# Attention and two MoE layers on one core: keys and queries loaded in 2 KB pieces, keys of two heads laid side by side on the chip, another order in the last step

## The chip, the cores and the metric

One core of one Trainium2 chip. The metric is the device time of one execution in microseconds (us); what stands for a kernel is the median of its runs. The core's engines are PE (matrix products), DVE (vector), ACT (scalar and activation), POOL (general) and SP (here it only issues transfers); 16 DMA engines move data.

## The reference, cut to what matters

Inputs q, k and v have the shape (2, 8, 768, 64): 2 batches, 8 heads, 768 positions, 64 numbers a head. All is float32.

```
k_sum = max of k over blocks of 32 positions        # 24 a head
v_sum = mean of v over blocks of 32 positions
scores_l = q @ k.T / 8, kept where |i - j| < 16
scores_s = q @ k_sum.T / 8 + log(32)
a = softmax over [scores_l, scores_s];  attn = a @ [v, v_sum]
x = attn as (1536, 512)
p = domain_probs / row sum
x = sum over 4 experts of p[:, e] * (relu(x @ w1[e]) @ w2[e])
P = 8 rounds of row and column scaling of exp(x @ w_gate - max)
out = sum over 8 experts of P[:, e] * (relu(x @ w1b[e]) @ w2b[e])
```

w1 has the shape (512, 1024) for each expert, w2 (1024, 512). The output has the shape (1536, 512).

## The kernel before, in words

**Attention.** The 16 heads are taken as 8 pairs (`pairs`). For pair i, `add_loads` (L1024) issues on SP: k of both heads (L1031), q of both heads (L1038), v (L1045), and windows of v (L1057). K lands with a position a partition, so a run of 256 B; q with two positions a partition, 512 B. There are two buffers for each of k, q and v, used in turn. `add_keys` (L1067) turns k over on PE (7 transposes of 128 columns, two halves of which one block is common), so that both heads' 64 numbers lie on 128 partitions and positions along the columns; ACT copies one half into `kw`, DVE the other (L1097 to L1101): 12 tiles of 96 positions, overlapping, each followed by 24 columns for the block maxima. DVE takes the maxima (L1106) and spreads them over the tiles (L1120). `add_queries` (L1130) turns q over and writes the scaled queries into `bd`, every second column for each of the two positions of a partition (L1147). `add_values` (L1160) makes the block means of v on POOL and PE. `add_group` (L1195) does 4 tiles at a time: scores on PE, maximum on DVE, exponentials on ACT, sum on DVE, product with 1/sum on POOL (L1250), transposes on PE, their copy on ACT, product with v on PE, and the copy into the layer's input `xf`. There are 24 such groups. `add_x` (L703) makes from `xf` the seven operands of the first product, each split in two parts (hi on ACT, L463; lo on DVE or POOL, L458 and L453).

**MoE.** A unit is 256 of an expert's 1024 hidden columns; there are 16 units in the first layer and 32 in the second, and for each unit two steps, b = 0 and 1, one for each batch: 96 steps. A step has a first product (`add_first`, L510; matmuls L303), a hop in which the hidden values become seven split operands (`add_hop`, L564), and a second product (`add_second`, L603; matmuls L612) that is added into `acc`. Each product uses seven products of quarter blocks in place of eight, named by digits: `FIRST` and `SECOND` (L1368, L1369) give their order for each b. Digit 2 is A12 B21, 3 is S4 B22, 4 is A22 N4, 7 is S3 T3. Each of the seven is 6 matmuls in the first product and 3 for each half dc in the second. `add_weights` (L465) loads a unit's weights, sums blocks of them by accumulating DMAs from POOL (L498) and splits them. At the border between the layers `add_turn` (L735) makes the next input; after expert 0 of the second layer `add_scale` (L769) applies its weights. `add_out` (L911) adds up, turns over and stores.

**Order.** Nothing runs in the order of the text. Each piece is an `op` (L358) with an engine, a planned time from `SPAN` (L330), what it reads and writes, and a due time. `run_work` (L377) plays all engines forward with these times and always emits the piece that can start first, the smaller due time deciding among equals. That fixes the order on every engine, SP and POOL queues included. Instructions marked `shared` (SBUF to SBUF on DVE and POOL) are planned one at a time. Constants at L1370 to L1386 shift due times: `ALONG` for the attention as a whole, `AHEAD` for its loads, `W0DUE` and `WAIT0` for the first unit's weights, `LEAD2` for the splits, `SOONER` and `LATER` for the steps about the border, `NARROW` for the pair from which three PSUM banks are left to the MoE.

Of the kernel before, what the change touches and what calls it, by code (L numbers as in the profile page):

```python
# [18 lines left out]
def local_global_attention_moe_moe(  # L19
# [14 lines left out]
    P = 128  # L34
# [98 lines left out]
    PB = [xp.tile([P, BLK], F32, name=f"pb{b}") for b in range(2)]  # L133
# [10 lines left out]
    KT = 7  # L144
    KA, KB = KT * KX, (NQ - KT) * KX
# [12 lines left out]
    def view_vs(t):  # L158
        return t.rearrange("x (t j d) -> x t j d", j=2, d=D)

    kns = [
        t.rearrange("x (c j d) -> x c j d", j=2, d=D)
        for t in (quads[:, 0:BLK], put("h0", BLK, "kn"))
    ]
    qns = [
        t.rearrange("x (j c d) -> x j c d", j=2, d=2 * D)
        for t in (quads[:, BLK:2 * BLK], put("h1", BLK, "qn"))
    ]
    vns = [t.rearrange("x (h c d) -> x h c d", h=2, d=D) for t in (PB[1], put("h2", BLK, "vn"))]
# [10 lines left out]
    ks = [accs[1][:, 2 * NB_ + i * NS:2 * NB_ + (i + 1) * NS] for i in range(2)]  # L180
    vbs = [accs[1][0:KX, 2 * NB_ + (i + 1) * P:2 * NB_ + (i + 2) * P] for i in range(2)]
# [17 lines left out]
    HOP_AT = {B11: "h0", N1: "h1", B21: "h2", B22: "h3", N2: "h3", T3: "h5", N4: "h5"}  # L199
# [15 lines left out]
    def x_of(b, c, r, i):  # L215
        if (b, c) != (1, 1):
            return xop[b, c][r][:, i]
        if (i, r) not in x11:
            tag = X_AT[i]
            group = [x for x in range(NOP) if X_AT[x] == tag]  # L220
            if tag == "xc":
                x11.update(operand("x11c", tag, group, (0, 1)))
            else:
                x11.update(operand(f"x11{tag}{r}", f"{tag}{r}", group, (r,)))
# [91 lines left out]
    def relu(S, out, src, th, neg=False):  # L316
# [12 lines left out]
    ADD = 0.85  # L329
# [6 lines left out]
        "v1536": (1.3, 1.34), "vmax": (0.57, 0.65), "vsum": (0.57, 0.66), "vrec": (0.12, 0.18),  # L336
        "vks": (0.6, 0.69), "vksw": (0.600001, 0.69), "vks2": (0.35, 0.42), "vkw": (0.7, 0.81), "vq": (1.0, 1.1),
# [4 lines left out]
        "p256": (0.75, 0.77), "p384": (1.05, 1.08), "psm": (0.98, 1.02), "pks": (0.8, 0.85),  # L342
        "pid": (0.55, 0.6), "p1": (0.2, 0.25), "pmask": (3.0, 3.1), "psel": (0.9, 0.95),
        "add1": (0.95, 1.3, ADD, 1.2), "add2": (0.950001, 1.3, 2 * ADD, 1.2),
        "addx": (0.950003, 1.3, 1.5 * ADD, 1.2), "add3": (0.950002, 1.3, 3 * ADD, 1.2), "ld": (0.45, 1.0, 0.65, 1.3),
        "st": (0.450001, 0.5, 0.5, 1.2), "ldk": (0.550002, 1.1, 1.2, 1.2),
# [256 lines left out]
    def add_second(n):  # L603
# [897 lines left out]
```

## Time and profile before

| | us |
|---|---|
| median of 3 runs | 1543.28 (1543.21 to 1543.91) |
| the profiled execution's own time | 1539.3 |
| its span, first to last instruction | 1537.3 |
| busy: PE, DVE, ACT, POOL | 1507.2, 1373.2, 1137.7, 486.1 |
| granted PE clock, mean | 0.999 of full |

Each row of a window gives its length, for every engine the busy time and in brackets the number of instructions, the granted clock, the busy share of the 16 DMA engines (it can be over 1, since packets overlap) and GB/s. In a row by line `out<-in` names the tiles, then come partitions x elements; behind the bar stand busy us and the mean of one in ns. The chain of waits follows the work that ended last back to what released it.

### The profile page before, as it was taken

Reading aid. Unit: us, or ns where it says so; the run is one execution under the profiler, and the core shown is the slowest. Engines: PE = TensorE matmul, PEld = TensorE weight load, DVE = VectorE, ACT = ScalarE, POOL = GpSimd, SP = SyncE. Lnnn points to the kernel's source line nnn. Section 1 sums busy time; section 2 is a strip of 40 time slices with the busy share of each in tenths; the row PEclk is TensorE's granted clock in tenths of the full one; section 3 lists DMA queues with packets and bytes.
Section 4 is the critical chain, followed back from the end, with each engine's and each line's share of the span. In section 5 each row is a group of like instructions: output and inputs, shape, how many; then the busy total and the mean of one; then the engine's idle time right before and its main releaser. Section 6 shows DMA issues by size and latency. Waiting matters only on the chain.

```text
span 1537.3 us, 26618 instructions
## 1 busy us (share of the span) xinstructions
PE 1507.2 (98%) x9058; PEld 1481.4 (96%) x9058; DVE 1373.2 (89%) x2842; ACT 1137.7 (74%) x2443; POOL 486.1 (32%) x513
## 2 busy tenths in 40 slices
PE   7989999999999999999999999999999999999997
PEld 6889999999999988998999999999999999999996
DVE  7987999899889896999989899899899899899987
ACT  5988777777677788767677677677777777777764
POOL 4643323323322341343232323323332323233220
PEclk9999999999999999999999999999999999999999
DMA  9977666566566683597567566667567566567632
GB/s 216 230 131 141 123 132 129 112 131 130 107 133 134 111 156 70 102 173 150 100 121 149 106 122 140 114 119 142 110 124 144 106 126 139 111 120 136 120 62 89
DMA packets 199032, 196.51 MB, mean 128 GB/s; under 512 B 46432, under 2 KB 157424, under 8 KB 198896
## 3 DMA queue, kind: packets, MB, share of 16 engines
q0 software_dynamic: 82944, 116.42, 47.6%
q1 hardware_dynamic: 115952, 78.39, 18.5%
q8 instruction: 71, 1.16, 0.3%
q14 instruction: 65, 0.53, 0.1%
HBM read 73.97 MB, written 3.22 MB: 50 GB/s over the span
## 4 chain that ended last, share of the span: by engine, by line
PE 89%; DVE 5%; DMA 2%; ACT 2%; POOL 1%; issue 1%; SPq 0%; DVEq 0%; POOLq 0%; ACTq 0%
PE bank L303 44%; PE bank L612 43%; DVE acc L238 1%; DVE hoph L458 1%; DMA pb<-prow 1%; PE bank L800 0%; ACT s L1235 0%; DVE acc L244 0%; POOL s L1250 0%; ACT xhi L463 0%; DMA pb<-in_v_dram 0%; DMA raw<-in_moe_w_dram 0%; DMA raw<-raw 0%; DMA acc<-acc 0%; DVE quads L320 0%
## 5 line engine op out<-in xcount | busy, mean ns | idle before, releaser
L612 PE MATMUL bank<-hoph,w2hi 128*128 128x384 f32 x2688 | 687.8, 336 | 7.4 <-ACT bank L623 5.8
L612 PEld LDWEIGHTS bank<-hoph,w2hi 128*128 128x128 f32 x2688 | 483.5, 188 | 14.2 <-ACT bank L623 9.8
L612 PE MATMUL bank<-hoph,w2lo 128*128 128x384 f32 x1344 | 449.5, 334 | 0.0
L238 DVE TENSOR_TENSOR acc<-bank,acc 128x384 f32<-128x384 f32 x730 | 386.4, 553 | 14.9 <-PE bank L612 13.1
L463 ACT ACTIVATE hoph<-quads 128x384 fp32r<-128x384 f32 x672 | 335.0, 522 | 61.5 <-PE bank L612 36.8
L458 DVE TENSOR_TENSOR hoph<-quads,hoph 128x384 fp32r<-128x384 f32 x583 | 313.1, 555 | 36.7 <-ACT hoph L463 36.6
L303 PE MATMUL bank<-xhi,w1hi 128*128 128x384 f32 x1008 | 338.6, 336 | 1.9 <-DVE quads L320 1.9
L303 PE MATMUL bank<-xlo,w1hi 128*128 128x384 f32 x1008 | 337.3, 335 | 0.0
L303 PE MATMUL bank<-xhi,w1lo 128*128 128x384 f32 x1008 | 337.0, 334 | 0.0
L498 POOL DMA_DIRECT2D raw<-raw x195 | 198.5, 1029 | 363.6 <-DMA raw<-raw 146.6
L623 ACT COPY bank<-bank 128x384 f32<-128x384 f32 x384 | 180.9, 471 | 116.0 <-PE bank L612 110.2
L612 PEld LDWEIGHTS bank<-hoph,w2lo 128*128 128x128 f32 x1344 | 252.3, 188 | 0.2 <-DMA w2lo<-xf 0.2
L303 PEld LDWEIGHTS bank<-xhi,w1hi 128*128 128x128 f32 x1008 | 189.2, 188 | 3.9 <-DVE quads L320 2.6
L303 PEld LDWEIGHTS bank<-xhi,w1lo 128*128 128x128 f32 x1008 | 189.2, 188 | 0.1
L303 PEld LDWEIGHTS bank<-xlo,w1hi 128*128 128x128 f32 x1008 | 189.3, 188 | 0.0
L498 POOL DMA_DIRECT2D xf<-xf x93 | 95.7, 1029 | 176.3 <-DMA xf<-xf 75.1
L623 ACT COPY bank<-acc 128x384 f32<-128x384 f32 x174 | 83.5, 480 | 86.0 <-DVE acc L238 84.9
L623 ACT COPY acc<-bank 128x384 f32<-128x384 f32 x218 | 103.7, 481 | 47.6 <-PE bank L612 43.2
L491 POOL DMA_DIRECT2D w2lo<-raw x66 | 69.7, 1056 | 182.4 <-ACT w2lo L488 178.3
L320 DVE SCALAR_TENSOR_TENSOR quads<-bank,pb 128x384 f32<-128x384 f32 x178 | 99.0, 556 | 21.9 <-PE bank L303 16.2
L582 DVE SCALAR_TENSOR_TENSOR quads<-quads 128x384 f32<-128x384 f32 x192 | 106.3, 554 | 1.5
L241 DVE TENSOR_TENSOR quads<-quads 128x384 f32<-128x384 f32 x185 | 102.6, 555 | 2.0 <-ACT quads L318 0.5
(190 smaller groups left out, 1904.1 us busy)
## 6 DMA issues: line engine op xcount, KB each, us to landing
raw<-raw POOLq DMA_DIRECT2D x130, 256.0 KB, 4.0
raw<-in_moe_w_dram SPq DMA_DIRECT2D x66, 256.0 KB, 2.8
raw<-in_moe_w_dram SPq DMA_DIRECT2D x128, 128.0 KB, 3.1
xf<-xf POOLq DMA_DIRECT2D x62, 256.0 KB, 3.8
w2lo<-raw POOLq DMA_DIRECT2D x33, 384.0 KB, 4.8
w1lo<-raw POOLq DMA_DIRECT2D x32, 384.0 KB, 4.0
pb<-prow SPq DMA_DIRECT2D x24, 384.0 KB, 3.8
w2lo<-raw POOLq DMA_DIRECT2D x33, 256.0 KB, 3.8
```

The source lines that it names most:

```text
L238: (eng or nc.vector).tensor_tensor(out=out, in0=x, in1=y, op=ALU.add)
L241: (eng or nc.vector).tensor_tensor(out=out, in0=x, in1=y, op=ALU.subtract)
L303: nc.tensor.matmul(pm, l[:, s, cs_], x_of(b, c, r, x), start=first and i == 0, stop=i == n - 1, skip_group_check=True,)
L320: nc.vector.scalar_tensor_tensor(out=out, in0=src, scalar=0.0, in1=PB[S[1]][:, th * HB:(th + 1) * HB], op0=ALU.min if neg else ALU.max, op ...
L458: e.tensor_tensor(out=out, in0=src, in1=hi.bitcast(F32), op=ALU.subtract)
L463: aop(lambda: nc.scalar.mul(to(0), src, -1.0 if neg else 1.0), reads, writes, due, "ah")
L491: lambda: nc.gpsimd.dma_start(out=l, in_=src, accum_op=ALU.add),
L498: lambda o=o, x=x: nc.gpsimd.dma_start(out=o, in_=x, accum_op=ALU.add),
L582: nc.vector.scalar_tensor_tensor(out=q[o], in0=q[x], scalar=-1.0, in1=q[y], op0=ALU.mult, op1=ALU.subtract)
L612: nc.tensor.matmul(cut[bank], l[:, s, cols], hop_of(t, r), start=start and i == 0, stop=i == 2, skip_group_check=True,)
L623: aop(lambda: nc.scalar.copy(out=out, in_=src), [kin], [kout], due)
```

## The change

K is loaded as q and k lie in memory, 8 positions (2 KB) a partition on 96 partitions, into one staging buffer `kst`; two copies, on DVE for the first pair and on POOL for the others, lay the two heads side by side in `kn`; PE makes 8 transposes of 96 columns, in two halves of 4; ACT copies one half to `kw` and DVE the other. Since a transposed column block holds every 8th position, the copies write every 8th element. The maxima are taken in two halves, and one instruction merges and spreads them. Q is loaded likewise, turned over in 2 x 4 transposes of 96 columns and scattered with the same step. `kst`, `kn` and `qn` have one buffer each. `kn` lies in the place of the two weighting rows `pb`, v's first buffer moves to `quads`, and the operand N1 of the hop moves from `h1` to `h0`.

Further: b = 1 gets other orders in `FIRST` and `SECOND`, the second product of the last step the order `FINAL`; one subtraction of `add_turn` for each half (b = 1, operand 6) goes to POOL; planned times and due times change, which changes the order everywhere. `BYPOOL` is empty, so its two branches never run. The diff, cut:

```diff
+    pbs = xp.tile([P, 2 * BLK], F32, name="pb")
+    PB = [pbs[:, b * BLK:(b + 1) * BLK] for b in range(2)]
...
+    RW = 8
+    RP, NR = S // RW, 2 * RW * D
...
+    kst = put("h0", NR, "kst")[0:RP].rearrange("x (j r d) -> x j r d", j=2, d=D)
+    kn = pbs[0:RP, 0:NR].rearrange("x (r j d) -> x r j d", j=2, d=D)
+    qn = quads[0:RP, 0:NR].rearrange("x (j r d) -> x j r d", j=2, d=D)
...
-    ADD = 0.85
+    ADD = 1.0
...
-        "st": (0.450001, 0.5, 0.5, 1.2), "ldk": (0.550002, 1.1, 1.2, 1.2),
+        "ld": (0.45, 1.0, 0.65, 1.3), "ldr": (0.55, 1.1, 1.75, 1.3),
+        "st": (0.450001, 0.5, 0.5, 1.2), "ldk": (0.550002, 1.1, 0.57, 1.2),
...
-    HOP_WAIT = 0.09
+    HOP_WAIT = 0.08
...
-            for j, m in enumerate(SECOND[b]):
+            for j, m in enumerate(SECOND[b] if n < NST - 1 else FINAL):
...
-                lo_op("DVE", to, src, [key, k + (0,)], [k], d, neg)
+                eng = "POOL" if (b, i) in TURNPOOL and not neg else "DVE"
+                lo_op(eng, to, src, [key, k + (0,)], [k], d, neg)
...
-                    out=kn[:, :, j, :], in_=k[b, 2 * hp + j].rearrange("(c p) d -> p c d", p=P)
+                    out=kst[:, j], in_=k[b, 2 * hp + j].rearrange("(p r) d -> p r d", r=RW)
...
-                    in_=q[b, 2 * hp + j].rearrange("(c p r) d -> p c (r d)", p=P, r=2),
+                    out=qn[:, j], in_=q[b, 2 * hp + j].rearrange("(p r) d -> p r d", r=RW)
...
+            op(
+                "POOL" if i and KPOOL[j] else "DVE", "pkj" if i and KPOOL[j] else "vkj",
+                [("kst", j)],
+                [("kn", j)], d - 0.01,
+                lambda j=j: (nc.gpsimd if i and KPOOL[j] else nc.vector).tensor_copy(
+                    out=kn[:, :, j], in_=kst[:, j]
+                ),
+                True,
+            )
...
+                for r in range(n):
+                    nc.tensor.transpose(
+                        full[tk["bank"]][:, r * RP:(r + 1) * RP],
+                        kn[:, r0 + r].rearrange("x j d -> x (j d)"), ident[0:RP, 0:RP],
+                    )
...
+                copy = nc.vector.tensor_copy if half else nc.scalar.copy
+                to = t[:, :, 0:KW].rearrange("x t (m r) -> x t r m", r=RW)
+                w = KW // RW
+                for src, st, tiles in (
+                    ((QT - WIN) // RW, QT // RW, slice(1, NQ - 1)),
+                    (0, (S - KW) // RW, slice(0, NQ, NQ - 1)),
+                ):
+                    o = to[:, tiles, r0:r0 + n, :]
...
+            a, b_ = (x[:, None, :].to_broadcast([P, NQ, NS]) for x in ks[p])
+            nc.vector.tensor_tensor(out=t[:, :, KW:KX], in0=a, in1=b_, op=ALU.max)
...
-                        t[j * D:(j + 1) * D, :, j, r:QT:2],
+                        t[j * D:(j + 1) * D, :, j].rearrange(
+                            "x t (q c r) -> x r c t q", r=2, c=RW // 2
+                        )[:, r],
...
-    FIRST = {0: "1562734", 1: "1567342"}
-    SECOND = {0: "1256437", 1: "1524637"}
-    HOP, GOFF, DCOFF, LEAD, LEAD2 = 1.11, 0.15, 6.7, 1.0, 0.94
+    FIRST = {0: "1562734", 1: "1567234"}
+    SECOND = {0: "1256437", 1: "1526437"}
+    FINAL = "1562743"
+    HOP, GOFF, DCOFF, LEAD, LEAD2 = 1.11, 0.15, 6.7, 1.0, 0.53
...
-    AHEAD = 3.8
-    ALONG = 7.5
-    NARROW = 7
-    WAIT0 = 1
-    KSPOOL = False
-    XDUE = [-2.5, -1.7, -0.9, 0.3]
-    W0DUE = -4.8
-    FIRST0 = -1.3
+    BYPOOL = ()
+    ALONG = 5.2
+    NARROW = 6
+    WAIT0 = 3
+    KPOOL = (True, True)
+    AHEAD, VAT, SAT = 6.3, 0.3, 0.86
+    XDUE = [-2.6, -1.7, -0.9, -0.5]
+    W0DUE = -2.1
+    FIRST0 = 0.2
...
+    TURNPOOL = ((1, 6),)
```

`LATER`, `SOONER` and `XPOOL` get other values too, and more of the planned times.

## Rows read from the trace of the kernel before

**Rows 1.** Busy time of each engine, page, part 1: us, share of span.

```profile
PE 1507.2 (98%) x9058; PEld 1481.4 (96%) x9058; DVE 1373.2 (89%) x2842; ACT 1137.7 (74%) x2443; POOL 486.1 (32%) x513
```

**Rows 2.** Windows of the second MoE layer: length, busy us (instructions), clock, DMA.

```profile
700.00:720.00 20.00, 18.92 (x105) 17.60 (x104) 19.92 (x43) 14.27 (x30) 7.23 (x8) 1.00 0.84 162
740.00:760.00 20.00, 20.00 (x117) 20.00 (x116) 18.68 (x38) 16.84 (x37) 4.69 (x5) 1.00 0.57 122
```

**Rows 3.** Windows of the attention, same columns.

```profile
0.00:30.00 30.00, 21.55 (x177) 18.29 (x178) 20.44 (x49) 15.36 (x41) 12.40 (x30) 1.00 1.08 212
30.00:60.00 30.00, 29.38 (x325) 26.08 (x324) 27.50 (x70) 28.11 (x83) 18.40 (x19) 1.00 1.12 240
60.00:90.00 30.00, 24.51 (x301) 20.88 (x299) 27.85 (x61) 25.30 (x74) 19.81 (x21) 1.00 0.94 176
90.00:110.00 20.00, 19.41 (x145) 18.00 (x146) 18.25 (x34) 18.45 (x41) 6.62 (x7) 1.00 0.69 131
```

**Rows 4.** Chain of waits, 0 to 110 us: start us, us, what.

```profile
26.38 5.21 DMA raw<-in_moe_w_dram
31.61 3.95 DMA acc<-in_v_dram
...
85.22 5.08 DMA raw<-raw
```

**Rows 5.** Timeline of PE, same stretch: start, us, line, [idle before].

```profile
4.77 1.73 PE L1077 MATMUL bank<-ident,quads 128*128 128x128 f32 x7 [4.77 <-POOL sel L985]
...
89.92 0.44 PE L303 MATMUL bank<-xhi,w1hi 128*128 128x384 f32 x1
```

**Rows 6.** DMA issues, 0 to 100 us: count, KB each, median us to landing.

```profile
quads<-in_k_dram SPq DMA_DIRECT2D x8, 192.0 KB, 5.0
```

**Rows 7.** DMA packets of 8-10, 2-4, 28-30, 31-33, 1522.5-1526 us; last line: queue.

```profile
DMA packets 1400, 0.35 MB, mean 176 GB/s; under 512 B 1400, under 2 KB 1400, under 8 KB 1400
DMA packets 1762, 0.50 MB, mean 248 GB/s; under 512 B 1552, under 2 KB 1762, under 8 KB 1762
DMA packets 763, 0.57 MB, mean 287 GB/s; under 512 B 44, under 2 KB 763, under 8 KB 763
DMA packets 684, 0.61 MB, mean 305 GB/s; under 512 B 60, under 2 KB 497, under 8 KB 684
DMA packets 491, 0.92 MB, mean 264 GB/s; under 512 B 47, under 2 KB 47, under 8 KB 490
q1 hardware_dynamic: 490, 0.91, 69.2%
```

**Rows 8.** DVE by line, 0 to 92 us: shapes, count | busy, mean ns.

```profile
L1147 DVE TENSOR_SCALAR bd<-bank 64x384 f32<-64x384 f32 x8 | 4.4, 546 | 0.1
L1097 DVE COPY kw<-bank 128x384 f32<-128x384 f32 x4 | 2.2, 550 | 0.4 <-PE bank L1077 0.4
L458 DVE TENSOR_TENSOR xlo<-acc,xhi 128x384 fp32r<-128x384 f32 x6 | 4.5, 747 | 1.3 <-ACT xhi L463 1.3
L453 DVE SCALAR_TENSOR_TENSOR xlo<-acc,xhi 128x384 fp32r<-128x384 f32 x1 | 0.5, 544 | 0.0
```

**Rows 9.** POOL by line, 0 to 92 us.

```profile
L1250 POOL TENSOR_TENSOR s<-s,sm 128x480 f32<-128x480 f32 x24 | 25.0, 1056 | 28.9 <-DVE sm L1245 13.8 <-ACT acc L1285 5.3 <-ACT s L1265 3.2
L238 POOL TENSOR_TENSOR pb<-pb 128x384 f32<-128x384 f32 x4 | 4.5, 1135 | 2.7 <-DMA pb<-in_v_dram 2.7
```

**Rows 10.** ACT by line, 0 to 92 us.

```profile
L1147 ACT ACTIVATE bd<-bank 64x384 f32<-64x384 f32 x8 | 4.1, 515 | 1.3 <-PE bank L1139 1.1
L1097 ACT COPY kw<-bank 128x576 f32<-128x576 f32 x4 | 2.6, 661 | 5.2 <-PE bank L1077 3.8 <-DVE acc L1106 1.4
```

**Rows 11.** Chain of waits, 1490 to 1538 us.

```profile
1511.10 0.56 DVE quads L320
...
1516.37 0.99 ACT hoph L463 x2
...
1528.65 0.53 DVE acc L629
```

More of the change, by code (lines that the diff above doesn't have):

```diff
@@ L481, in group @@
             aop(lambda: nc.scalar.copy(out=h, in_=src), rd, [key + ("hi",)], due, span)
+            if (kind, u) in BYPOOL:
+                op(
+                    "POOL", f"p{n * FU}", rd + [key + ("hi",)], [key + ("lo",)], due + 0.05,
+                    lambda: vsub(l, src, h.bitcast(F32), nc.gpsimd), True,
+                )
+                return
             if by_dve:
@@ L495, in add_weights @@
         for o, x, wr, rd in sums_of(kind, u):
+            if (kind, u) in BYPOOL:
+                op(
+                    "POOL", f"p{len(wr) * FU}", [R[j] for j in (*rd, *wr)], [R[j] for j in wr],
+                    start + 0.5, lambda o=o, x=x: vadd(o, o, x, nc.gpsimd), True,
+                )
+                continue
             op(
@@ L906, in add_row @@
         op(
-            "SP", "ld", [f"prow{layer + 1}"], keys, due,
+            "SP", "ldr", [f"prow{layer + 1}"], keys, due,
             lambda: load_row(out, layer, e, b),
@@ L1103, in maxima, with copies @@
-            def maxima(half=half, c0=c0, nh=nh, tk=tk):
+            op("PE", "kt4", [("kn", 0), ("kn", 1), "ident"], key, e, turn, take=tk)
+            def copies(half=half, r0=r0, tk=tk):
+                pt = full[tk["bank"]]
+                copy = nc.vector.tensor_copy if half else nc.scalar.copy
[6 more added lines that the diff above has]
+                    o = to[:, tiles, r0:r0 + n, :]
+                    copy(
+                        out=o,
+                        in_=bass.AP(
+                            pt.tensor, pt[:, src:src + 1].offset,
+                            [list(pt.ap[0]), [st, o.shape[1]], [RP, n], [1, w]],
+                        ),
+                    )
@@ L1115, in add_keys @@
                 vop(copies, key, [("kw", p, 1)], e, "vkw", False, use=tk)
[L1116 removed]
+            vop(maxima, key, [("ks", p, half)], e, "vks", False, use=tk)
         def spread():
[L1119 to L1128 removed]
+            a, b_ = (x[:, None, :].to_broadcast([P, NQ, NS]) for x in ks[p])
+            nc.vector.tensor_tensor(out=t[:, :, KW:KX], in0=a, in1=b_, op=ALU.max)
+        vop(spread, [("ks", p, 0), ("ks", p, 1)], [("kw", p, 2)], d + 0.03, "vksw", True)
     def add_queries(i, d):
@@ L1350, in set_places @@
         for key in QUAD:
-            over[key] = [(x, 0, j) for x in ("kn", "qn") for j in range(2)]
-        over["pb", 1] = [("vn", 0)]
+            over[key] = [("qn", 0), ("qn", 1), ("vn", 0)]
         for i in range(NOP):
@@ L1418, in local_global_attention_moe_moe @@
                     add_x(b, c, XDUE[i // 2])
+        for b in range(2):
+            over["pb", b] = [("kn", 0), ("kn", 1)]
         op(
-            "SP", "ld", ["prow1", ("mark", 4)], [("pb", 0)], A0 + 14 * AD,
+            "SP", "ldr", ["prow1", ("mark", 4)], [("pb", 0)], A0 + 14 * AD,
             lambda: load_row(PB[0], 0, 0, 0),
```

131 lines of the change are left out of this document (50 added, 81 removed), and 2 rows, old and new, of the table SPAN.

## Prediction

> **What bounds the kernel now.** I read the page's busy shares first, then the windows by stage, then the chain of waits, then the DMA view, and last the groups by line of the engines that the change touches.
>
> The busy shares put PE at 98% of the span [rows 1], but that is an average over stages. The windows show them apart. A full stretch of the MoE has PE at 20.00 of 20 us with 117 matmuls [rows 2]; nothing that spares DMA, DVE or ACT can shorten it. Time can be won only where PE runs short: in the attention at the front, around the border between the layers and at the weighting step of the second layer, and in the tail.
>
> In the attention PE, DVE and the DMA engines share the blame. From 0 to 110 us DVE is busy 94.04 us, so it sits idle for 15.96 us; 9.56 us of that lies in the first 30 us, 4.65 us in the next 60 [rows 3]. DMA stands at 94 to 112% of the 16 engines over the first 90 us [rows 3] (above 100% because packets overlap on an engine). So the loads gate the first third, and DVE (27.5 and 27.9 us of 30) the other two. The chain of waits says the same: three of its longest pieces in this stage are transfers, one of them the weights of the first unit, loaded between the third and the fourth pair of heads, with a window load of v behind it, and one the sum of that unit's weights, which ends just after the first MoE product has started at 89.92 us [rows 4, 5].
>
> **Part 1: K and Q in 2 KB pieces.** Each of the 16 K and 16 Q issues moves 192 KB, K rows of 256 B and Q rows of 512 B (one of four such rows is shown [rows 6]): 6.29 MB in 18432 packets; afterwards 3072 packets of 2 KB. The rate before: a stretch with nothing but 256 B packets moves 176 GB/s, one with mostly K from 256 B rows 248 GB/s, one with 512 B and larger pieces 287 GB/s [rows 7]. K's 3.15 MB thus take 12.7 to 17.9 us; Q's 3.15 MB lie between 248 and 287 GB/s, 11.0 to 12.7 us. Together 23.7 to 30.6 us. The rate after: nearest are a stretch with 2 KB weight rows among others, 305 GB/s, and the stores of 2 KB rows, 0.92 MB in 3.5 us with a third of the stretch idle, so at 69.2% busy some 380 GB/s [rows 7]. That gives 16.6 to 20.6 us. The saving in transfer time is 3.1 to 14.0 us; I take 9, near the middle, because the windows that run beside the K loads are the 256 B kind and slow them. The saving is on the path as long as the transfers gate, which is the first third and parts of the rest.
>
> **Part 2: the copy that lays two heads side by side.** Two copies of 512 elements for each pair. For the first pair they run on DVE: with 0.55 us for 384 elements [rows 8], 0.73 us each, 1.5 us in all, on the path of the first transposes; K landing sooner and PE's start, which now waits on POOL's mask work until 4.77 us [rows 5], cover about 1 us. For the other seven pairs POOL does them: 14 copies. The nearest rows are POOL's two-operand instructions of 384 and 480 elements, 1.14 and 1.06 us [rows 9]; I take 1.1 us, 15 us in all. POOL is busy 50.6 of the first 90 us [rows 3], so they fit, up to 66. What they cost is contention: where POOL works beside it, DVE's subtraction takes 747 ns, its like 544 ns [rows 8]. Six rows at 0.2 us over their like are 1.2 us; 15 us on top of POOL's 50.6 raise that by a third, and other DVE lines have their share, so 0.4 to 2 us; I take 1. Behind a copy that waits for its K stand on POOL the products of the softmax (24 of 1.06 us [rows 9]), for which PE's transposes wait. Only one K stage and one Q buffer remain, so the next load can't start until the copy, or Q's transposes, are through; a K transfer lands 5.0 us after issue [rows 6] and a pair takes some 10 us, so I take 0, with up to 2 us as the bound.
>
> **Part 3: the scatter on the chip.** PE turns 8 + 8 blocks of 96 columns where it turned 7 + 6 of 128: 1536 columns for 1664, nothing. The maxima read 768 columns as before (2 x 384 for 512 + 256). DVE's share of the keys grows from 480 to 576 columns, 96/384 of 0.55 us, 0.14 us for each pair, and the spread becomes one instruction instead of two; I take 0. The copies of keys and the scaled queries now write every 8th element, 32 B apart, where keys were contiguous and queries 8 B apart. The trace prices the 8 B step: 384 elements take 546 ns with it and 550 ns without on DVE, and on ACT 515 ns with it [rows 8, 10]. A step of 32 B is not in it. Its cost lies between 0 and a doubling of those rows; I take 0, since the only stepped rows at hand cost nothing. The doubling is the third rival.
>
> **Part 4: order.** The first unit's weights wait for the fourth pair's K (WAIT0 3) and are due later, which takes the piece at 26.38 us out of the attention's way [rows 4]. What is late next is their sums: already now their last transfer ends only as the first products run [rows 4, 5]. Part of the 5 us won at 26 us may be given back there; I leave both inside the sum below. The dues of row loads, of POOL's accumulating DMAs and of the splits also move everywhere, which in the full stretches can gain nothing and lose up to 2 us.
>
> **Part 5: border and weighting.** DVE is busy 19.92 of 20 us while PE makes 105 matmuls instead of 117 [rows 2]. Two subtractions of 0.55 us go from DVE to POOL at the border: at most 1.1 us; I take 0.5, between 4 gained and 4 lost for the new order.
>
> **Part 6: the tail.** In the last step PE runs dry at 1511.1, when the gate of the product A12 B21 starts; all hop operands hang on it, and from there DVE and ACT work until 1517.4 [rows 11]. With the new order two products of 1.04 us follow this gate instead of none, so the chain starts 2.1 us sooner. FINAL ends with c12, which needs one instruction before the transposes, instead of c22, which has one of 0.53 us [rows 11] and two more of such length behind it: up to 1 us. I take 2.5 of these 3.1; bounds 4.5 gained (the ACT copy that waits on a store goes too) and 1 lost.
>
> **The sum.** In the attention the gain is what DVE's idle 15.96 us can give back. Some of it must stay: the loads still start from nothing, and the softmax's chain is serial. I take half, 8.0 us, after the 1 us of part 2; transfers save about as much (9). So 8.0 + 0.5 + 2.5 = 11.0 us. The profiled execution has a time of 1539.3 us (its span is 1537.3), 4.0 us under the median of 1543.28; I take that offset as unchanged, so 1543.3 - 11.0 = 1532.3 us.
>
> **Rivals.**
> 1. *All idle goes.* With quick loads the first MoE products, which need only the first half of the pairs, fill PE while DVE finishes: 16.0 + 0.5 + 2.5 = 19.0 us, 1524.3 us. For it speaks that PE, too, has idle in the attention; against it, DVE's 27.9 of 30 us [rows 3].
> 2. *The loads were hidden.* From 30 us on DVE is the limit anyway [rows 3], or the weight sums hold the first product [rows 4]; only parts 5 and 6 remain: 3.0 us, 1540.3 us. Against it speaks the idle 9.56 us of the first 30.
> 3. *Slower: the 32 B step.* If a write with this step takes twice as long, DVE pays for 576 + 768 elements per pair, 3.5 x 0.55 = 1.93 us, 15.4 us over eight pairs, and ACT 0.66 + 2 x 0.515 = 1.69 us, 13.5 us [rows 8, 10]. Then the sum is -11.0 + 15.4 = +4.4 us, 1547.7 us; it turns at 11.0 us, a factor of 1.7. Against it speaks that the 8 B step is free; for it, that nothing wider was run here. The Trainium skill (SBUF — State Buffer, section on Door 1, the DMA port swizzle) bears on this: "So how far you can stride for free depends on dtype: 4 fp32, 8 bf16, 16 int8." By that rule a step of 8 elements pays and one of 2 doesn't; the free 8 B rows agree with it, but no row decides about 32 B; were its price the doubling, the time would be this rival's.
>
> **How the numbers follow.** Forecast 0.60, its own range 1527 to 1537; rival 1 0.15, rival 2 0.13, rival 3 0.12. About 0.2%, 3.1 us, is what a measurement of this kernel can tell from no change. Forecast and rival 1 are faster (0.75), rival 2 lies at the edge and counts as same (0.13), rival 3 is slower (0.12). The range 1524 to 1544 holds all but rival 3 and what lies below rival 1.
>
> **What would show it.** Right: the DMA view counts about 1536 packets each for K and Q; the DMA share in the first 80 us falls below 100%; DVE's idle in 0 to 110 us falls to about 8 us; the first product of L303 starts near 82 us instead of 89.92 [rows 5]; the last one before the final transposes comes some 2 us closer to the end. Wrong: the key copies and scaled queries take over 0.9 us for 384 elements (rival 3); the product starts after 87 us though the loads are through early (rival 2); the POOL copies stand waiting for K with softmax products behind them; PE falls under 117 matmuls per 20 us between 120 and 540 us.

## The result: slower, and the profile after

The changed kernel takes 1552.85 us (median of 5 runs, 1551.88 to 1560.63), the kernel before, run beside it on the same chip, 1543.71 us (5 runs, 1543.21 to 1544.54). The ratio is 1.0074, 95% interval 1.0055 to 1.0093: slower by 9.1 us by the medians and 11.4 by the ratio, where 11 us of gain were forecast. The profiled execution of after took 1551.88 us with a span of 1550.0 us.

The busy shares (page, part 1) hardly differ from [rows 1]:

```profile
PE 1512.8 (98%) x9082; PEld 1484.9 (96%) x9082; DVE 1372.6 (89%) x2835; ACT 1138.7 (73%) x2443; POOL 497.8 (32%) x528
```

As before, the answer lies in the stages. The windows of after, same columns as [rows 2, 3]:

```profile
0.00:30.00 30.00, 21.11 (x178) 18.50 (x178) 23.38 (x45) 16.86 (x38) 15.83 (x35) 1.00 1.00 208
30.00:60.00 30.00, 27.74 (x326) 24.15 (x324) 27.79 (x57) 27.33 (x74) 17.41 (x21) 1.00 1.03 230
60.00:90.00 30.00, 25.98 (x264) 22.65 (x262) 25.50 (x54) 26.14 (x63) 21.24 (x23) 0.89 0.84 174
90.00:110.00 20.00, 17.78 (x166) 14.98 (x162) 18.37 (x37) 17.38 (x47) 10.93 (x11) 1.00 0.51 102
...
740.00:760.00 20.00, 20.00 (x118) 20.00 (x117) 18.34 (x37) 14.07 (x30) 4.23 (x6) 1.00 0.50 93
840.00:860.00 20.00, 17.67 (x93) 17.34 (x92) 14.17 (x30) 12.31 (x26) 7.10 (x7) 0.91 0.66 125
```

Two things are to be seen. In the first 30 us DVE is 3 us busier than in [rows 3] and yet runs fewer instructions (45 for 49): its instructions got longer. And a stretch in the middle of the second layer, 840 to 860 us, has 93 matmuls where a full one has 117 [rows 2], at a granted clock of 0.91.

DVE, ACT and POOL by line, 0 to 95 us (columns as in [rows 8 to 10]); these answer to the key copies and scaled queries there:

```profile
L1115 DVE COPY kwxa<-bank 128x480 f32<-128x480 f32 x4 | 4.1, 1026 | 0.0
L1115 DVE COPY kwxa<-bank 128x96 f32<-128x96 f32 x4 | 1.4, 343 | 0.0
L1115 ACT COPY kwxa<-bank 128x480 f32<-128x480 f32 x4 | 4.2, 1061 | 1.3 <-DVE acc L1126 1.2
L1168 DVE TENSOR_SCALAR bd<-bank 64x384 f32<-64x384 f32 x8 | 6.8, 854 | 0.1
L1168 ACT ACTIVATE bd<-bank 64x384 f32<-64x384 f32 x8 | 6.9, 863 | 0.2
L1085 POOL COPY pb<-kst 96x512 f32<-96x512 f32 x14 | 8.6, 626 | 2.9 <-DMA kst<-in_k_dram 2.8
L1085 DVE COPY pb<-kst 96x512 f32<-96x512 f32 x2 | 0.8, 417 | 0.0
```

A scaled query of 384 elements takes 854 ns on DVE and 863 on ACT; with the 8 B step of before it took 546 and 515 [rows 8, 10]. That is 1.57 and 1.68 times. The copies that lay two heads side by side are cheap: 626 ns on POOL, 417 on DVE.

PE's timeline, 60 to 100 us: the first MoE product (L299, before L303) starts at 92.32 us, 2.4 us later than in [rows 5]:

```profile
68.46 2.06 PE L1236 MATMUL bank<-kwxa,acc 128*128 128x120 f32 x8 [1.56 <-DVE kwxa L1143]
...
92.32 0.33 PE L299 MATMUL bank<-xhi,w1hi 128*128 128x384 f32 x1
```

The DMA issues of 0 to 100 us, first after, then the rows of before that stand beside the one in [rows 6]:

```profile
kst<-in_k_dram SPq DMA_DIRECT2D x16, 192.0 KB, 5.1
quads<-in_q_dram SPq DMA_DIRECT2D x16, 192.0 KB, 4.1
```

```profile
quads<-in_q_dram SPq DMA_DIRECT2D x8, 192.0 KB, 4.4
...
kn<-in_k_dram SPq DMA_DIRECT2D x8, 192.0 KB, 6.5
qn<-in_q_dram SPq DMA_DIRECT2D x8, 192.0 KB, 4.6
```

The pieces are as planned: the page counts 183672 packets for 199032, and the difference of 15360 is exactly 18432 less 3072. The loads of the same 192 KB land little sooner: K 5.1 us after its issue (median), where it took 5.0 into one buffer and 6.5 into the other, Q 4.1 us, where it took 4.4 and 4.6.

**Where the time went.** I counted the matmuls of the two products (L299 and L621) up to a given moment in both traces; one takes 0.174 us. After lags before by 6.9 us at 120 us, 7.8 at 540, 7.5 at 720, 11.8 at 860, 15.3 at 1500, and the spans differ by 12.7. Between these two profiles the attention lost 7 us, the first layer and the border nothing more, the second layer's full stretches 7.8, and the tail gave 2.4 back: from the last first product to the end it is 23.88 us, before 26.23. One caution: the profiled execution of before was 4.0 us faster than its median, that of after 1.0, so some 3 us of this lag are those of the two executions. Two kernels that are as fast as before by their medians (2 and 3 below) show where they lie: counted alike, the profile of b_order lags 1.9 us at 120 us, that of b_kq1536 2.8, and their first products start at 91.97 and 92.85 us. So 4 to 5 of the attention's 7 us belong to the change, and a first product at 92.32 us is no sign of a loss by itself.

The waits of 720 to 1480 us (engine, buffer and line, what it waited for: us in total, times, longest us) show what stops the second layer; before had no wait of PE there, and none of ACT's splits for a sum:

```profile
ACT w1hi L478 <- DMA raw<-raw: 7.5, 5, 3.1
...
PE bank L621 <- ACT bank L632: 4.8, 5, 2.3
ACT w1hi L478 <- DMA xf<-xf: 1.6, 1, 1.6
```

and the timeline at 840 us shows one of them:

```profile
840.33 1.20 POOL L507 DMA_DIRECT2D raw<-raw  x1 [3.96 <-DMA raw<-raw]
...
844.22 0.62 ACT L478 CAST w1hi<-raw 128x512 fp32r<-128x512 f32 x1 [3.10 <-DMA raw<-raw]
844.87 0.69 DVE L237 TENSOR_TENSOR w1lo<-raw,w1hi 128x512 fp32r<-128x512 f32 x1 [2.54 <-ACT w1hi L478]
845.49 0.47 ACT L632 COPY bank<-bank 128x384 f32<-128x384 f32 x1
...
846.01 0.96 PE L621 MATMUL bank<-hoph,w2hi 128*128 128x384 f32 x2 [2.33 <-ACT bank L632]
```

POOL stood 3.96 us for one sum before it issued the next; the split of the weights on ACT waited 3.10 us for that one; and behind the split, in ACT's order, stood the bank copy for which PE's second product waits, 2.33 us. The split itself is not urgent, but it blocks the queue. PE's waits make 5.1 of the 7.8 us. Right behind this wait the granted clock is 0.76 and 0.81 in the 8 us from 844 us, which by estimate (the missing share of each 4 us) is up to 1.7 us more.

### The profile page after: what moved, and what is told of

Read it like the earlier page. It is cut to its first block, busy times and chain, and to the rows that moved or that the text cites. A ratio compares the mean times of both kernels' runs of the same rounds, so it can differ in the third digit from the quotient of the medians.

```text
span 1550.0 us, 26653 instructions
## 1 busy us (share of the span) xinstructions
PE 1512.8 (98%) x9082; PEld 1484.9 (96%) x9082; DVE 1372.6 (89%) x2835; ACT 1138.7 (73%) x2443; POOL 497.8 (32%) x528
## 2 busy tenths in 40 slices
DMA packets 183672, 196.51 MB, mean 127 GB/s; under 512 B 34144, under 2 KB 138992, under 8 KB 183536
## 5 line engine op out<-in xcount | busy, mean ns | idle before, releaser
L621 PE MATMUL bank<-hoph,w2hi 128*128 128x384 f32 x2688 | 686.7, 336 | 10.9 <-ACT bank L632 8.9
L621 PEld LDWEIGHTS bank<-hoph,w2hi 128*128 128x128 f32 x2688 | 483.4, 188 | 18.9 <-ACT bank L632 15.1
L621 PE MATMUL bank<-hoph,w2lo 128*128 128x384 f32 x1344 | 449.8, 335 | 0.3 <-DMA w2lo<-xf 0.3
L507 POOL DMA_DIRECT2D raw<-raw x195 | 192.2, 988 | 495.1 <-DMA raw<-raw 319.6
L299 PE MATMUL bank<-xhi,w1hi 128*128 128x384 f32 x1008 | 338.6, 336 | 4.4 <-DVE quads L237 2.6
L299 PE MATMUL bank<-xhi,w1lo 128*128 128x384 f32 x1008 | 337.2, 334 | 0.0
L299 PE MATMUL bank<-xlo,w1hi 128*128 128x384 f32 x1008 | 337.0, 334 | 0.0
L455 DVE TENSOR_TENSOR hoph<-quads,hoph 128x384 fp32r<-128x384 f32 x583 | 307.4, 549 | 5.5 <-ACT hoph L460 5.2
L621 PEld LDWEIGHTS bank<-hoph,w2lo 128*128 128x128 f32 x1344 | 252.6, 188 | 0.7 <-DMA w2lo<-xf 0.7
L299 PEld LDWEIGHTS bank<-xhi,w1hi 128*128 128x128 f32 x1008 | 189.4, 188 | 6.7 <-DVE quads L237 3.1
L299 PEld LDWEIGHTS bank<-xhi,w1lo 128*128 128x128 f32 x1008 | 189.4, 188 | 0.3 <-DVE w1lo L237 0.3
L299 PEld LDWEIGHTS bank<-xlo,w1hi 128*128 128x128 f32 x1008 | 189.4, 188 | 0.0
L532 ACT ACTIVATE quads<-bank 128x384 f32<-128x384 f32 x192 | 94.0, 491 | 20.9 <-PE bank L299 16.0
```

What stands on the lines that cost most here:

```text
L299: nc.tensor.matmul(pm, l[:, s, cs_], x_of(b, c, r, x), start=first and i == 0, stop=i == n - 1, skip_group_check=True,)
L455: e.tensor_tensor(out=out, in0=src, in1=hi.bitcast(F32), op=ALU.subtract)
L507: lambda o=o, x=x: nc.gpsimd.dma_start(out=o, in_=x, accum_op=ALU.add),
L532: aop(lambda: nc.scalar.mul(out, src, by), [kin], [kout], due)
L621: nc.tensor.matmul(cut[bank], l[:, s, cols], hop_of(t, r), start=start and i == 0, stop=i == 2, skip_group_check=True,)
```

## The experiments

The theory after the result: **the 32 B step** made the attention slower (rival 3's mechanism at a smaller factor), the faster transfers gave nothing (rival 2), and **the planned times** of the sums cost the second layer's stalls. The rivals: the loss comes from the new order alone, or from the single buffers, which no run undoes. Each kernel ran beside the kernel before on the same chip; of the four batches before had medians of 1543.60, 1542.33, 1543.15 and 1542.66 us, so kernels of different batches are compared by their ratios.

### 1. Undo the step (a_loop)

The same elements go to the same places, but the innermost loop runs over the positions that lie together on the writing side: keys in runs of 4 neighbours, queries 8 B apart. The wide step (96 columns, 384 B) falls on the read from PSUM.

```diff
-                to = t[:, :, 0:KW].rearrange("x t (m r) -> x t r m", r=RW)
+                to = t[:, :, 0:KW].rearrange("x t (m r) -> x t m r", r=RW)
...
-                    o = to[:, tiles, r0:r0 + n, :]
+                    o = to[:, tiles, :, r0:r0 + n]
...
-                            [list(pt.ap[0]), [st, o.shape[1]], [RP, n], [1, w]],
+                            [list(pt.ap[0]), [st, o.shape[1]], [1, w], [RP, n]],
...
-                            "x t (q c r) -> x r c t q", r=2, c=RW // 2
+                            "x t (q c r) -> x r t q c", r=2, c=RW // 2
...
-                            "x (c t q) -> x c t q", c=RW // 2, t=NQ
+                            "x (c t q) -> x t q c", c=RW // 2, t=NQ
```

> In the kernel after, the copies of keys and of scaled queries run over the same elements in another loop order: keys are written in runs of 4 neighbours, queries 8 B apart, and the wide step moves to the read from PSUM (384 B). Theory C (the 32 B step of the write is what made the 384-element query write 0.855 us instead of 0.546): it falls to 0.55 to 0.60 us on DVE and ACT, the keys likewise, DVE and ACT win about 8 us of work each, the first MoE product starts 3 to 6 us sooner and the time falls to about 1548 us. Rival (any scattered access costs, on whichever side): the writes stay at 0.85 us or above and the time at 1552 us or more.

Measured: 1543.22 us (10 runs, 1539.01 to 1549.22), ratio 1.0002 (0.9985 to 1.0019). The lines of 0 to 95 us:

```profile
L1168 DVE TENSOR_SCALAR bd<-bank 64x384 f32<-64x384 f32 x8 | 4.4, 552 | 1.3 <-PE bank L1156 1.2
L1168 ACT ACTIVATE bd<-bank 64x384 f32<-64x384 f32 x8 | 4.1, 514 | 0.7 <-PE bank L1156 0.6
L1115 DVE COPY kwxa<-bank 128x480 f32<-128x480 f32 x4 | 2.6, 647 | 0.0
L1115 ACT COPY kwxa<-bank 128x480 f32<-128x480 f32 x4 | 2.3, 577 | 1.0 <-DVE acc L1126 1.0
```

The price is gone, on both engines and for both kinds of copy: 854 to 552 ns, 1026 to 647. A step on the reading side costs nothing that these rows show. The whole loss of the change goes with it, 9.6 us by the medians, 11 by the ratios, and the first product starts at 85.57 us. But the forecast gain does not appear: the kernel is level with before. (In this execution the lag at 1500 us is still 7.5 us, and three splits still wait 4.8 us for sums.)

### 2. The loads alone (b_kq1536)

The kernel before with K and Q in pieces of 1536 B instead of 256 and 512 B: every partition takes 6 consecutive rows. The positions are permuted by this, so the kernel attends to other positions than the reference; all instructions and bytes are the same.

```diff
-                    out=kn[:, :, j, :], in_=k[b, 2 * hp + j].rearrange("(c p) d -> p c d", p=P)
+                    out=kn.rearrange("x c j d -> x (c j d)")[:, j * (BLK // 2):(j + 1) * (BLK // 2)],
+                    in_=k[b, 2 * hp + j].rearrange("(p r) d -> p (r d)", p=P)
...
-                    out=qn[:, j],
-                    in_=q[b, 2 * hp + j].rearrange("(c p r) d -> p c (r d)", p=P, r=2),
+                    out=qn[:, j].rearrange("x c d -> x (c d)"),
+                    in_=q[b, 2 * hp + j].rearrange("(p r) d -> p (r d)", p=P),
```

> The kernel before, with K and Q loaded in runs of 1536 B (6 rows a partition, 128 partitions) into the same places; nothing else moves. The rows land in another order, so what is left out is the right order of keys and queries; all instructions and bytes stay. Theory E (the small pieces gate the attention): DMA's share over the first 80 us falls from 1.09 to about 0.95 and the time by 3 to 8 us, to about 1538 us. Rival (the loads are hidden behind DVE, ACT and PE): within 1.5 us of before.

Measured: 1542.52 us against 1542.33, ratio 0.9999 (0.9991 to 1.0008). Its windows:

```profile
0.00:30.00 30.00, 21.38 (x170) 17.65 (x171) 19.53 (x45) 14.43 (x39) 12.40 (x30) 1.00 0.95 219
30.00:60.00 30.00, 29.41 (x315) 25.97 (x316) 27.49 (x72) 28.05 (x81) 17.48 (x18) 1.00 1.04 244
```

The DMA engines are less busy, 0.95 and 1.04 for 1.08 and 1.12 [rows 3], and move 3 and 2% more bytes per second. The time doesn't move. So the transfers were hidden: a DMA share above 100% did not mean that anybody waited for them. The trace of before could have said so: of the waits of all its engines in 0 to 110 us only one group of 0.2 us or more is for a K or Q transfer:

```profile
POOL s L1250 <- DMA quads<-in_k_dram: 0.5, 1, 0.5
```

The Trainium skill (DMA: Bandwidth & Descriptors, Specifications) gives "≥512 B" as the smallest transfer for line rate; the lower share agrees with it, but a rate that nobody waits for is worth nothing here.

### 3. The new order alone (b_order)

The kernel before with the change's `FIRST` and `SECOND` for b = 1 and `FINAL`.

```diff
-    FIRST = {0: "1562734", 1: "1567342"}
-    SECOND = {0: "1256437", 1: "1524637"}
+    FIRST = {0: "1562734", 1: "1567234"}
+    SECOND = {0: "1256437", 1: "1526437"}
+    FINAL = "1562743"
...
-            for j, m in enumerate(SECOND[b]):
+            for j, m in enumerate(SECOND[b] if n < NST - 1 else FINAL):
```

> The kernel before with nothing but the new FIRST and SECOND for b = 1 and FINAL for the last step. Theory D (the new order shortens the tail and does nothing else): 2 to 3 us less than before, about 1541 us, all of it after 1500 us. Rival (the order costs in every step with b = 1): PE falls under 117 matmuls per 20 us in the full stretches, 1544 us or more.

Measured: 1543.54 us, ratio 1.0001 (0.9990 to 1.0011); the tail 25.62 us for 26.23. Not the rival's loss, and not the gain either. The timelines show what lies on top of the order in this tail. First ACT and PE of this kernel:

```profile
1528.88 0.58 ACT L941 COPY xf<-bank 128x512 f32<-128x512 f32 x1 [1.23 <-DMA out_dram<-xf]
...
1529.90 0.62 PE L612 MATMUL bank<-hoph,w2hi 128*128 128x384 f32 x2 [1.47 <-ACT bank L623]
...
1531.87 4.40 PE L929 MATMUL bank<-ident,acc 128*128 128x128 f32 x23 [0.54 <-DVE acc L238]
```

and PE's last row in after, which has no wait for a store:

```profile
1542.00 2.73 PE L939 MATMUL bank<-ident,acc 128*128 128x128 f32 x23 [0.54 <-DVE acc L234]
```

A copy of ACT into the output's buffer waits 1.23 us until an earlier store has left it, the bank copy behind it comes late, and PE waits 1.47 us. From the last first product to these transposes it is 17.19 us, in after 15.88. The transposes take 4.40 us for 2.73, since the granted clock is 0.57 in 1532 to 1536, but from their start to the end it is 8.43 us for 8.00, so the clock costs the end only 0.4. The store's wait is the larger part of the 1.7 us by which this tail is longer than after's.

That wait does not belong to the order. Here are before and, in the last row, c_att (see 6), whose last step has before's order:

```profile
1526.25 0.59 ACT L941 COPY xf<-bank 128x512 f32<-128x512 f32 x1 [1.47 <-DMA out_dram<-xf]
...
1527.27 0.61 PE L612 MATMUL bank<-hoph,w2hi 128*128 128x384 f32 x2 [1.70 <-ACT bank L623]
```

```profile
1527.49 0.61 PE L621 MATMUL bank<-hoph,w2hi 128*128 128x384 f32 x2 [0.55 <-ACT bank L632]
```

In c_att's timelines no copy in the tail waits for a store, and the tail is 25.18 us for 26.23. So of the 2.4 us between before and after the orders have about 1.3 (25.18 to 23.88), the store the rest; what removes the store's wait was not shown. The time of the whole kernel shows no gain from the order (see 8).

### 4. The planned times (a_lead94, a_add85, b_add)

a_lead94 is the change with the lead of the second layer's operands as before:

```diff
-    HOP, GOFF, DCOFF, LEAD, LEAD2 = 1.11, 0.15, 6.7, 1.0, 0.53
+    HOP, GOFF, DCOFF, LEAD, LEAD2 = 1.11, 0.15, 6.7, 1.0, 0.94
```

> Only LEAD2 goes back from 0.53 to 0.94 in the kernel after. Theory A (the splits S1 and S4 are now put into ACT's queue before the sums they read have landed, and what stands behind them there holds PE): the 9 to 10 us that PE loses between 120 and 540 us and between 720 and 1480 us go, the waits of ACT for the sums' DMAs there fall from 11 us to under 2, and the time falls to about 1544 us. Theory B (the planned DMA times, ADD and the rest, are what misplaces them): no change, 1552 us within 2 us, the stalls stay.

Measured: 1549.20 us, ratio 1.0035 (1.0018 to 1.0052). ACT's waits for sums in 720 to 1480 us fall from 7.5 to 3.6 us, PE's for the bank copy from 4.8 to 1.7. The time lies between the two theories, 3.6 us under after's by the medians, and its interval just under after's: the lead seems to be a part of the loss, and not all of it.

a_add85 is the change with the planned durations of the sums as before; b_add is the kernel before with those of the change (the same lines, the other way round):

```diff
-    ADD = 1.0
+    ADD = 0.85
...
-        "add1": (0.95, 1.3, ADD, 1.1), "add2": (0.950001, 1.3, 1.8 * ADD, 1.1),
-        "add3": (0.950002, 1.3, 2.3 * ADD, 1.1), "addx": (0.950003, 1.3, 1.4 * ADD, 1.1),
+        "add1": (0.95, 1.3, ADD, 1.2), "add2": (0.950001, 1.3, 2 * ADD, 1.2),
+        "addx": (0.950003, 1.3, 1.5 * ADD, 1.2), "add3": (0.950002, 1.3, 3 * ADD, 1.2),
...
-    HOP_WAIT = 0.08
+    HOP_WAIT = 0.09
```

> In the kernel after, ADD, the four accumulating-DMA times and HOP_WAIT go back to their values before; LEAD2 stays at 0.53. Theory B: the stalls in the full stretches go, about 1544 us. Theory A: they stay, 1552 us within 2 us, since the due time still places the splits too early.

> The kernel before with ADD 1.0, the new add1 to add3 and addx and HOP_WAIT 0.08. Theory B (these planned times make the stalls): PE falls under 117 matmuls per 20 us in several full stretches, ACT waits for the sums' DMAs, 1547 to 1550 us. Rival (they do so only together with LEAD2 0.53 and the new order of b = 1): no change, 1543.6 us within 1.5.

Measured: a_add85 1550.60 us, ratio 1.0050 (1.0033 to 1.0067); b_add 1548.80 us, ratio 1.0040 (1.0027 to 1.0053). In a_add85 the second layer's stalls are gone, as its waits of 720 to 1480 us show beside those of after:

```profile
ACT w1hi L478 <- DMA raw<-raw: 0.4, 1, 0.4
...
PE bank L621 <- ACT bank L632: 0.2, 1, 0.2
```

Its lag is 10.4 us at 720 us and 10.8 at 1500. So the planned durations do make those stalls, but most of what is won there was lost at the start: 9.9 us behind at 120, after 6.9. By the intervals its time is not told apart from after's. In b_add the same constants cost 6.5 us, though not in the second layer: it is 5.7 us behind at 120 us and 8.9 at 1500, with 0.2 us of waits of PE from 720 to 1480. Its PE timeline has one place, a first product that waits behind ACT's bank copy right after the start of the MoE (before's longest wait in 80 to 112 us is 0.93 us):

```profile
88.23 0.65 PE L1259 MATMUL bank<-ident,s 128*120 128x128 f32 x4 [1.14 <-POOL s L1250]
...
93.94 0.45 PE L303 MATMUL bank<-xhi,w1hi 128*128 128x384 f32 x1 [2.27 <-ACT bank L523]
```

The granted clock is 0.79 in 92 to 100 us. The constants cost 6.5 us, and they do it by the order that the planner derives from them, at another place in each kernel; no single place can be named.

### 5. Both repairs (c_best)

The change with the edits of a_loop and a_add85 together, no other.

> The kernel after with two edits together: the loop order of the scattered copies (keys in runs of 4, queries 8 B apart) and the planned DMA times ADD, add1 to add3, addx and HOP_WAIT as before. If the two causes are separate (the step holds the attention, the planned DMA times make the stalls in the full stretches) their gains add: 9 us from the first and about 5 us more, so 1538 us, under both kernels. If the planned DMA times only shift stalls about, or the a_loop run owed its time to chance, 1543 us.

Measured: 1544.13 us (13 runs, 1540.58 to 1555.08), ratio 1.0011 (1.0001 to 1.0022): not below a_loop. The prices of the two edits don't add up. Its profiled execution took 1555.08 us, 11 us over the median, and shows the blocked queue of ACT once more, here with a low clock behind it (0.50 in 1320 to 1324 us). Its timeline, all engines, 1312 to 1320 us:

```profile
1316.40 0.62 ACT L478 CAST w1hi<-xf 128x512 fp32r<-128x512 f32 x1 [3.59 <-DMA xf<-xf]
...
1318.19 1.01 PE L621 MATMUL bank<-hoph,w2hi 128*128 128x384 f32 x2 [2.83 <-ACT bank L632]
```

### 6. The new attention alone, without the step (c_att)

c_best with what lies outside the attention put back as it was before.

```diff
-    FIRST = {0: "1562734", 1: "1567234"}
-    SECOND = {0: "1256437", 1: "1526437"}
-    FINAL = "1562743"
-    HOP, GOFF, DCOFF, LEAD, LEAD2 = 1.11, 0.15, 6.7, 1.0, 0.53
+    FIRST = {0: "1562734", 1: "1567342"}
+    SECOND = {0: "1256437", 1: "1524637"}
+    HOP, GOFF, DCOFF, LEAD, LEAD2 = 1.11, 0.15, 6.7, 1.0, 0.94
...
-    LATER = {1: 0.2, 2: 0.6, 3: 1.0, 8: 0.2}
-    SOONER = {-2: 0.2, -1: -0.4, 0: 1.0, 1: -0.2, 2: 0.2, 3: -0.2, 6: -0.2, 7: 0.4, 8: 1.0}
+    LATER = {-2: -0.2, 1: 0.2, 2: 0.8, 3: 1.0, 8: -0.2}
+    SOONER = {-2: 0.6, -1: -0.4, 0: 1.0, 1: -0.2, 2: 0.2, 3: 0.2, 6: 0.4, 7: 1.0}
...
-    TURNPOOL = ((1, 6),)
+    TURNPOOL = ()
```

(`FINAL` at its place of use goes too, and the planned costs `vs` and `ldr` are those of before.)

> As c_best, but everything that isn't the attention goes back to the kernel before: FIRST, SECOND, no FINAL, LEAD2, LATER, SOONER, TURNPOOL, the planned times of row loads and of the small DVE pieces. What is left of the change is the attention with 2 KB loads, POOL copies and a cheap scatter. If the larger pieces are worth what the forecast says, the first MoE product starts near 83 us and the time is about 1538 us without the tail's gain of 2.4; if the loads were hidden it is 1543 us or more.

Measured: 1540.10 us (10 runs, 1538.61 to 1544.69), ratio 0.9987 (0.9977 to 0.9996). This beats both kernels, by 2.2 us over before. What still bounds its attention is DVE, with PE's waits for Q: DVE is busy 95.9 us of the first 110, idle 14.1 for 15.96 [rows 3]. Of PE's waits of 0 to 125 us the longest group is:

```profile
PE bank L1156 <- DMA quads<-in_q_dram: 8.1, 3, 5.1
```

and the chain of waits of 0 to 92 us has two of them (start us, us, what):

```profile
5.12 0.89 PE bank L1156 x4
6.03 4.69 DMA quads<-in_q_dram
10.76 0.90 PE bank L1156 x4
...
53.60 5.81 DMA quads<-in_q_dram
```

The longest of the three waits, 5.1 us, is the start of the kernel, where before waited 4.77 us for the mask work [rows 5]; the other two make 3.0 us. The chain has the next Q transfer from 6.03 us, 0.02 us after the transposes that free a part of Q's only buffer, and PE waits for its end. Before, with two buffers for Q, PE waited for no Q transfer in the first 110 us.

### 7. The step put back (d_step), and the head copies on DVE (d_pool)

d_step is c_att with the loops of 1 in the change's order (the diff of 1 reversed). d_pool is c_att with

```diff
-    KPOOL = (True, True)
+    KPOOL = (False, False)
```

> The fastest kernel so far (new attention with the copies in runs of 4 elements, everything else as before, 1540.1 us) with one thing put back: the inner loop of the key copies and of the scaled queries steps 32 B again, as in the change. Theory (the step itself is what costs, by 1.6 times on DVE and ACT): in the change, undoing it gave 9.6 us, so here it costs 7 to 10 us again, 1547 to 1550 us; 384 elements at 850 to 870 ns on both engines, first MoE product 6 to 8 us later than 86.88. Rival (most of the 9.6 us came from the plan of the change, which the late attention only upset): 2 to 4 us, 1542 to 1544 us.

> The fastest kernel so far with the 14 copies that lay two heads side by side on DVE instead of POOL. Theory (DVE is the limit of the attention from 30 us on, POOL has room): 14 copies of 0.42 us, 5.8 us on DVE, of which half to all shows: 1543 to 1546 us. Rival (the copies on POOL slow DVE's neighbours and hold up the softmax products by as much): within 1 us of 1540.1 us.

Measured: d_step 1546.17 us, ratio 1.0023 (1.0014 to 1.0031), against c_att's 0.9987: 0.0036, 5.6 us. That lies between the two expectations, under the theory's 7 and above the rival's 4. The first product starts at 93.32 us, c_att's at 86.88, and the rows have the same price as in after:

```profile
L1168 DVE TENSOR_SCALAR bd<-bank 64x384 f32<-64x384 f32 x8 | 6.8, 849 | 0.1
L1168 ACT ACTIVATE bd<-bank 64x384 f32<-64x384 f32 x8 | 6.9, 866 | 0.2
L1115 DVE COPY kwxa<-bank 128x480 f32<-128x480 f32 x4 | 4.1, 1016 | 0.0
```

So the step costs 5.6 us where the order around it is before's, and 9.6 (by the medians; 11 by the ratios) in the change. The first is the price of the step by itself; why it costs more in the change was not shown. That a late attention meets an order with less slack there is a guess.

d_pool: 1544.24 us, ratio 1.0010 (1.0001 to 1.0019), 0.0023 or 3.5 us over c_att: as the theory had it. The copies take DVE 457 ns each there, so 14 of them add 6.4 us, and over half of that shows. POOL is the right engine for them.

### 8. The new order in the better kernel (d_tail, e_final)

d_tail is c_att with the diff of 3; e_final is c_att with `FINAL` alone.

> The fastest kernel so far with the change's orders FIRST and SECOND for b = 1 and FINAL added, its other constants still those of before. Theory (the order itself shortens the tail by the 2.4 us seen in the change): 1537.7 us, tail after the last first product 23.9 us instead of 25.2. Rival (in the kernel before the same three orders gave 0.2 us and a tail only 0.6 us shorter, so the tail's gain hangs on LATER, SOONER and TURNPOOL too): 1539.5 to 1540.3 us, tail 24.6 us or more.

> The fastest kernel so far with FINAL alone added: the order of the second product in the last step; FIRST and SECOND for b = 1 as before. Theory (with all three orders the tail got 1.3 us shorter, 25.18 to 23.87 us, and the border between the layers lost about as much, 2.4 us more behind at 720 us; FINAL touches only the last step): the tail's 1 to 1.3 us without the border's loss, 1538.8 to 1539.5 us against 1540.1, ratio to the kernel before about 0.998. Rival (the tail needs the new FIRST order ahead of it, or the gain is given back in the output's transposes and stores): tail over 24.8 us and no gain, ratio 0.9985 to 0.999.

Measured: d_tail 1540.46 us, ratio 0.9988 (0.9979 to 0.9997); e_final 1540.29 us, ratio 0.9986 (0.9976 to 0.9997); c_att 0.9987. No gain in either, so both theories fall in the time. In the traces the tail is shorter: 25.18 us in c_att, 24.29 in e_final, 23.87 in d_tail. From 540 to 720 us, about the border, d_tail's profile loses 2.4 us against before, c_att's 0.7 and e_final's 0.8, so d_tail may lose there what it wins at the end. But that is one execution, with a granted clock of 0.81 and 0.76 in 572 to 580 us, where those of the other two are full, and b_order loses 0.2 us there with the same orders; so it isn't shown. For e_final, which touches the last step alone, its 0.9 us is below what the runs can tell (the interval is 3 us wide).

## Why the prediction was wrong, point by point

Forecast were 11 us of gain, measured 9.1 of loss. Without the step the kernel is level with before (a_loop). So about half of the 20 us between is the step's cost, which the sum put at nothing, and half the 11 us of gain, none of which came.

**Part 3 failed first: "Its cost lies between 0 and a doubling of those rows; I take 0, since the only stepped rows at hand cost nothing."** The 8 B rows were the nearest, and they were the wrong neighbours. At 32 B the rows measure 1.57 times on DVE and 1.68 on ACT. For eight pairs DVE's copies and scaled queries (L1115, L1168) take 24.7 us for 16.0 in a_loop, 8.7 us more; ACT's about 25.7 for 15. Taking the step out gives 9.6 us, putting it into the better kernel costs 5.6. This was the third rival, with a chance of 0.12. Its doubling was too dear (15.4 us for 8.7), and at 8.7 us, below its turning point of 11, it would still have forecast a gain, because it left the 11 us standing.

The Trainium skill (SBUF — State Buffer, section on Door 1) was cited there and its rule held: "So how far you can stride for free depends on dtype: 4 fp32, 8 bf16, 16 int8." A run of 4 neighbours and a step of 2 elements are free here (647 and 552 ns), a step of 8 is not (1026 and 854 ns); a step of 4 was not run. By that rule the step should have been the likeliest case, at a price to be bounded, and not 0.

**Part 1 and the sum failed second: "I take half, 8.0 us … transfers save about as much (9)."** The transfers were shortened and it saved nothing: 1536 B pieces leave the time where it was (0.9999), and with 2 KB pieces a 192 KB load still takes 4.1 to 5.1 us to land. The step from "the DMA share is over 100%" to "so the loads gate the first third" was wrong. Rival 2 was right on this. The chain of waits that was to bear it out had three long transfers, but by its own rows a load of weights, a window of v and a sum of weights [rows 4]: none of them is a K or Q load, and no engine of before waited more than 0.5 us for one.

**Part 2** was right in kind: 626 ns for 1.1 us estimated on POOL, 417 ns for 730 on DVE, and POOL is worth 3.5 us over DVE (d_pool). The contention term had a weak source: the 747 ns [rows 8] are a mean of six, five of 0.54 to 0.62 us and one of 1.58, so nothing there shows 0.2 us for each; no run tells its cost. But of the single buffers it said "I take 0, with up to 2 us as the bound": without the step, PE waits 3.0 us for Q in two places behind the start (c_att). How much of this more buffers would give back wasn't tried.

**Part 4** took the weights of the first unit out of the way, and in c_att's chain of waits they are gone. But "in the full stretches can gain nothing and lose up to 2 us" was too small. After lost 7.8 us between 720 and 1500 us, for the larger part by splits that wait on ACT for sums and block the bank copies; with before's planned durations those stalls vanish (a_add85). The planned times cost 6.5 us in the kernel before (b_add). The mechanism, an engine's order that holds an urgent instruction behind a late one, was one of the things I had listed for other moves and not priced for this one.

**Part 5**: nothing is seen at the border in after (7.8 us behind at 540, 7.5 at 720); its 0.5 us can't be told. **Part 6** came out in size in the trace, 2.4 us for 2.5, but in part by luck: the orders have 1.3 of it, and the rest is the ACT copy that no longer waits on a store, which Part 6 had in its bound and not in its 2.5. As time it isn't shown: the orders alone moved nothing in three kernels (b_order, d_tail, e_final).

**The signs** named in advance read as follows. K and Q have 3072 packets; the DMA share of the first 80 us fell below 100%, from 1.09 to 0.95, and the tail got shorter, so these three signs of being right came true without a gain; but DVE's idle in 0 to 110 us is 15.0 us, not 8; the first product came at 92.32, not 82, past the 87 that was to speak for rival 2; 384 elements take 854 ns, just under the 0.9 us that was to speak for rival 3, a mark set too high; the POOL copies waited 2.8 us for K; and PE fell under 117 matmuls, to 107 in 220 to 240 us.

**What stays open.** Why the change's planned times cost 6.5 us in the kernel before but can't be told from nothing once the step is out (c_best against a_loop). Where c_att's 2.2 us come from: none of its parts was shown to give them. A part may lie in the tail: in the profiles of c_att, d_step and d_pool it is 25.13 to 25.18 us long, in those of the four kernels with before's attention (before, b_order, b_add, b_kq1536) 25.62 to 28.29, each with a copy of ACT that waits 1.2 to 2.3 us for a store.

## What to carry to other kernels

A scatter in fp32 from PSUM that wrote every 8th element took 1.6 times as long on DVE and 1.7 to 1.8 times on ACT; turn the loop so that the step falls on the read from PSUM and the write goes to near neighbours, which here cost nothing. A DMA share of 100% is no proof that transfers gate: ask which engine stands waiting for one, and whether it waits for rate, start or latency. And where a planner's numbers order the queues, a change of them is a change of the whole kernel and not of the stage that was meant: 6.5 us here where nothing else was changed (b_add).

## What the runs showed of the hardware

The price of a stepped write is similar on two engines that differ otherwise: some 310 ns more on DVE and 350 on ACT for 384 elements, 380 and 480 for 480; that is 0.8 ns an element on DVE and 0.9 to 1.0 on ACT.

TensorE's clock fell for short stretches in the profiles of all kernels but before, whose 4 us windows show none until the tail. In after the granted clock is 0.50 from 68 to 72 us, the lower of the two levels, right behind PE's wait of 1.56 us shown above, and the group of 8 matmuls then takes 2.06 us, elsewhere 1.05. Such dips stand in the profiles of a_loop, b_order, c_att and b_kq1536 too, at 56 to 88 us, and these kernels are as fast as before or faster; so they don't explain the change's loss, but they move single executions: b_order's, 0.75, 0.50 and 0.90 in 76 to 88 us, is by estimate up to 3.4 us of full clock.
